# Floors under the planner's due times of the early attention and weight pieces in a fused attention and two-layer feed-forward kernel

## The chip, the cores and the metric

The kernel runs on one core of one Trainium2 chip, in one launch. The time is device microseconds from the first to the last instruction with what lies around them; the figure that counts is the median of several executions.

## The reference

Attention in two directions over `x` (4 batches, 8 heads, 512 positions, 64 wide) and `state` (32 rows), then two feed-forward layers on the 4 x 544 = 2176 tokens of 512 channels. Cut to what matters:

```python
a = softmax(scale * x @ state.T);  xread = a @ state          # per batch and head
a2 = softmax(scale * state @ x.T); sread = a2 @ x
t = concat([xread, sread]) -> (2176, 512)
h = t @ w_in                       # 512 -> 2048
y = (h * tanh(softplus(h))) @ w_out               # 2048 -> 512
yn = y / rms(y) * rms_g
out = (silu(yn @ w_gate) * (yn @ w_val)) @ w_out2 # 512 -> 1536 -> 512
```

## The kernel before

Every product of the two layers is made in float16 pairs: a high part and a low part of each operand, three matmuls for one. The weights come from memory as float32 words in 1 MB halves ("load wi00" is the first half of unit 0 of `w_in`), through two staging buffers in `psm`. Vector and scalar engine turn each into scaled pairs: "hi", "s" (sign, L562), "l" (low words, L567/L569), "join" (L578), "sq" (a sum of squares, L599) for a scale by a tiny ones-matmul ("pow2", L481, six to seven tiny steps on DVE behind it), then "sh" and "sl" (the two halves, L610 by L468/L472 and L612). `w_in` and `w_out` are cut into four units of 512 hidden columns, wi0/wo0 to wi3/wo3. `plain` does one unit.

`attention(b)` makes the two reads of batch b, in two halves of four heads: x comes by eight DMAs of 128 KB (L707), PE transposes the state (L717) and x (L739, into one of four PSUM banks `p`), makes the scores (L752), DVE and ACT make two softmaxes (L761 to L791, the exponentials L768 and L773 on ACT), and PE makes the reads (L799), transposes (L814, L838) and the second product (L825). Batch 2 and 3 are needed late: their reads stand behind most of the first layer.

The first layer is done in groups, g0 to g8 (a batch by some units): `l1` is twelve 512-column matmuls into one bank (L926), followed on ACT by "mish" (L937), then "gh" and "gl" (L941) make the pair for `l2`, six matmuls for each of four column blocks d0 to d3 (L963) of a pair p of hidden blocks. g0 and g1 take unit 0 for batch 0 and 1, g2 and g3 unit 1, g4 and g5 units 2 and 3, g6 to g8 the batches 2, 3 and the state rows (as batch 4, with a scale from "x4"). While g4 and g5 run, `keep` begins to turn the nine units of the second layer's weights into a form that goes back to memory (L1375) through one 2048-word region; the next unit cannot be written into the region before the write out has been read off. The second layer (from about 411 us on) loads these back.

The order is not written by hand. Every step is an `Op` with its engines, cost and buffers; `Plan.order` gives each op a latest time (`chains`), runs a list scheduler by these times (`forward`), takes new latest times from the schedule it got (`backward`), and repeats this up to ten times, keeping the order whose modelled end was earliest. An op's `floor` is a lower bound for its latest time, taken from `P.floor` when the op is made:

```python
    o.floor = None if self.floor is None else self.floor()
    ...
    if o.floor is not None:
        late[o] = max(late[o], o.floor)
```

The second piece stands in `chains` alone; `backward` knows no floors. All engines then run their part of the order strictly in sequence.

Of the kernel before, what the change touches and what calls it, by code (L numbers as in the profile page):

```python
# [36 lines left out]
class Plan:  # L37
# [31 lines left out]
    def op(self, engs, fn, r=(), w=(), tab=None, at=None, reserve=0, lat=0.0, after=(), due=None, name=""):  # L69
        o = Op()  # L70
        o.engs, o.fn, o.tab, o.at, o.due, o.reserve, o.lat, o.name = engs, fn, tab, at, due, reserve, lat, name
        o.floor = None if self.floor is None else self.floor()
        o.succ, o.bufs = [], []
        deps = set(after)
        for n in r:
            if n in self.writer:
                deps.add(self.writer[n])
        for n in w:
            if n in self.writer:
                deps.add(self.writer[n])  # L80
            deps.update(self.readers.get(n, ()))
        for n in r:
            self.readers.setdefault(n, []).append(o)
        for n in w:
            self.writer[n] = o
            self.readers[n] = []
        for n in dict.fromkeys((*r, *w)):
            if n in self.pool_of:
                o.bufs.append(n)
                self.users[n] = self.users.get(n, 0) + 1  # L90
        deps.discard(o)
        o.deps = deps
        self.ops.append(o)
        return o
# [224 lines left out]
def attn_moe_moe_kernel(  # L319
# [23 lines left out]
    P = Plan(nc)  # L343
# [271 lines left out]
    def plain(w, u, m, at, xexp, pool="raw", after=()):  # L615

        def dst(k):
            return m(at + 256 + 512 * k, 512).rearrange("p (a f) -> p a f", a=2)

        def dn(k):  # L620
            return m.names(at + 256 + 512 * k, 512)

        fetch(w, u, dst, dn, pool, after)
        s = norms([(m(at + 256 + 1024 * i, 1024).rearrange("p (a n) -> p a n", a=2), [*dn(2 * i), *dn(2 * i + 1)])
                   for i in range(2)], (w, u), xexp, f"{w}{u}", 2)
        for k in range(4):
            split(m, at, k, s, ((w, u), "s"), f"{w}{u}")
# [322 lines left out]
    def flush():  # L950
        if pending:
            l2(*pending.pop(0))
# [453 lines left out]
    with tc.manual_schedule():  # L1406
        make_identity(nc, ident)
        nc.vector.memset(ones, 1.0)
        nc.vector.memset(rbias, -20.0 * LN2)
        op({"G": 1.6}, lambda e: nc.gpsimd.memset(sb[:, :B // 2], 0.0), w=["state"])  # L1410
        op({"V": 1.6}, lambda e: nc.vector.memset(sb[:, B // 2:], 0.0), w=["state"])
        held = [buf(("held", k), "t") for k in range(6)]
        op({"X": 0.01}, lambda e: None, w=held, name="hold")
        load_state()
        op({"T": 8.0 / 2}, rouse, w=["warm"], name="rouse")
        state_scale()
        attention(0)
        plain("wi", 0, *home["wi", 0], XEXP)
        attention(1)
        plain("wo", 0, *home["wo", 0], XEXP)  # L1420
        for u in range(1, U1):
            plain("wi", u, *home["wi", u], XEXP)
            plain("wo", u, *home["wo", u], XEXP)
        bar = op({"X": 0.01}, lambda e: None, w=["early"], after=list(early_raw), name="early")
        every = list(range(U1))
        group(0, 0, [0], None, 2)
        group(1, 1, [0], None, 3)
        group(2, 0, [1], 2, 2)
        group(3, 1, [1], 3, 3)
        group(4, 0, [2, 3], 2, 0)  # L1430
        flush()
        attention(2, clock[0] + DUE2)
        group(5, 1, [2, 3], 3, 1)
        flush()
        attention(3, clock[0] + DUE3)
        sread_scale(clock[0] + DUE3)
        done = op({"X": 0.01}, lambda e: None, r=held, after=list(att_ops), name="release")
        for w, u, k in (("wg", 0, 0), ("wv", 0, 0), ("wg", 1, 0), ("wv", 1, 1), ("wg", 2, 0), ("wv", 2, 1),
                        ("w2", 0, 1), ("w2", 1, 0), ("w2", 2, 1)):
            keep(w, u, k, [bar, done] if k else [bar])  # L1440
        conv = op({"X": 0.01}, lambda e: None, after=list(early_raw), name="conv")
        opened = []
        load("wg", 1, after=[done, conv])
        load("wv", 1, after=[done, conv])
        for u in range(U2):
            load("w2", u, after=[conv])
        gated_scales()
        group(6, 2, every, None, 2)
        flush()
        rms(0, slots_xe[0], [conv, done])  # L1450
        group(7, B, every, None, B)
        group(8, 3, every, None, 3)
        flush()
        load("wg", 0)
        load("wv", 0)
        opened.append(op({"X": 0.01}, lambda e: None, w=w2m.names(0, 7168), name="open"))
        opened.append(op({"X": 0.01}, lambda e: None, w=psm.names(4608, 1792), after=[conv], name="open"))
        P.floor = lambda: clock[0] - LATER
        gated()
        P.run()  # L1460
# [36 lines left out]
```

## Time and profile before

| | us |
|---|---|
| median of 3 runs (796.73 to 802.6) | 798.7 |
| the profiled execution, its own time | 801.31 |
| its span, first to last instruction | 799.5 |
| PE busy | 772.9 |
| DVE busy | 650.1 |
| ACT busy | 435.8 |
| first `l1` block on PE begins at | 48.02 |

The span is read as PE's time: what PE does not do, and what it does at the lower clock, is what an order can change.

### The profile page before, as it was taken

The page shows a single profiled execution, that of the slowest core. Times are in us where ns is not written, and L with a number is a line of the kernel's source. Part 1 is how long each engine was busy: PE and PEld are TensorE (multiplying, and loading weights), DVE is VectorE, ACT ScalarE, POOL GpSimd, SP SyncE. Part 2 cuts the span into 40 slices and gives each one's busy share as a digit, 9 for nine tenths or more (in the row PEclk, how much of TensorE's full clock was granted, in tenths as well). Part 3 has the DMA queues.
Part 4 walks back from the last instruction along what each step waited for, and adds up shares of the span by engine and source line. Part 5 has one row for each costly group of instructions (what it writes and reads, how often), then busy time and mean ns, then how long its engine had stood idle before and what let it go on. Part 6 is the DMA issues. An engine that isn't in the chain of part 4 may idle for free.

```text
span 799.5 us, 14253 instructions
## 1 busy us (share of the span) xinstructions
PE 772.9 (97%) x5830; PEld 528.0 (66%) x5830; DVE 650.1 (81%) x1332; ACT 435.8 (55%) x802; POOL 1.6 (0%) x7
## 2 busy tenths in 40 slices
PE   7699998999999999999999999999999999999997
PEld 5344454544344444774457588888888889889996
DVE  5989999998978798897689898668975998666671
ACT  6989998854746495776366543315530744122210
POOL 0000000000000000000000000000000000000000
PEclk9689999999999999999999999999999999999999
DMA  8663733202341543605353972368353745275001
GB/s 221 190 182 99 251 97 116 73 2 105 106 155 56 213 157 156 213 15 226 157 198 145 395 275 94 137 233 283 128 217 114 275 158 185 93 294 208 2 1 66
DMA packets 36885, 125.69 MB, mean 157 GB/s; under 512 B 20052, under 2 KB 20052, under 8 KB 30676
## 3 DMA queue, kind: packets, MB, share of 16 engines
q1 hardware_dynamic: 36820, 124.79, 44.0%
q8 instruction: 45, 0.74, 0.4%
q14 instruction: 20, 0.16, 0.1%
HBM read 101.45 MB, written 23.33 MB: 156 GB/s over the span
## 4 chain that ended last, share of the span: by engine, by line
PE 71%; DVE 16%; DMA 6%; ACT 6%; issue 1%; DVEq 0%; ACTq 0%; SPq 0%
PE p L1111 25%; PE a L963 14%; PE p L926 13%; PE a L1195 12%; DMA attm<-kept_wg 3%; PE p L1271 2%; ACT junk L599 1%; DVE g L941 1%; DVE w2m L612 1%; PE a L1309 1%; DVE sxm L562 1%; DVE page L507 1%; PE a L1403 1%; DMA kept_wg<-psm 1%; ACT sxm L567 1%
## 5 line engine op out<-in xcount | busy, mean ns | idle before, releaser
L963 PE MATMUL a<-g,w2m 128*128 128x512 f16 (+1 forms) x960 | 187.1, 349 | 1.1 <-DVE slot L807 0.8
L926 PE MATMUL p<-slot,w 128*128 128x512 f16 (+1 forms) x960 | 186.8, 350 | 0.3 <-ACT tt L937 0.3
L963 PEld LDWEIGHTS <-w2m 128*128 128x128 f16 x960 | 86.0, 99 | 90.9 <-issue 5.6
L926 PEld LDWEIGHTS <-w 128*128 128x128 f16 x960 | 86.3, 99 | 90.3 <-issue 4.1
L1111 PEld LDWEIGHTS <-w 128*128 128x128 f16 x1344 | 131.3, 98 | 17.0 <-issue 0.3
L1123 DVE TENSOR_TENSOR tt<-p,tt 128x512 f32<-128x512 f32 x120 | 82.3, 688 | 31.4 <-PE p L1111 30.4
L1111 PE MATMUL p<-slot,w 128*128 128x256 f16 x768 | 93.3, 273 | 0.0
L468 ACT ACTIVATE w2m<-tt 128x512 f16<-128x512 f32 x45 | 26.9, 623 | 93.0 <-DVE tt L1162 81.1
L1111 PEld LDWEIGHTS <-attm 128*128 128x128 f16 x672 | 65.4, 98 | 10.6 <-DMA attm<-kept_wg 2.2
L1195 PE MATMUL a<-attm,w2m 128*128 128x256 f16 x576 | 66.2, 273 | 0.0
L937 ACT ACTIVATE tt<-p,page 128x512 f32<-128x512 f32 x68 | 45.8, 678 | 32.4 <-PE p L926 32.2
L1195 PEld LDWEIGHTS <-w2m 128*128 128x128 f16 x576 | 56.3, 98 | 6.7 <-issue 0.2
L941 DVE SCALAR_TENSOR_TENSOR g<-tt,page,g 128x512 f16<-128x512 f32 x68 | 50.5, 747 | 2.0 <-ACT g L468 1.3
L1195 PE MATMUL a<-psm,g 128*128 128x256 f16 x432 | 51.9, 273 | 0.0
L1111 PE MATMUL p<-slot,attm 128*128 128x256 f16 x384 | 46.2, 273 | 1.6 <-DMA attm<-kept_wg 1.3
L1195 PEld LDWEIGHTS <-g 128*128 128x128 f16 x432 | 42.2, 98 | 5.6 <-issue 0.6
L1147 ACT ACTIVATE tt<-tt,page 128x512 f32<-128x512 f32 x36 | 25.6, 719 | 35.1 <-DVE tt L1123 35.0
L468 ACT ACTIVATE psm<-psm,page 128x512 f16<-128x512 f32 (+1 forms) x39 | 27.7, 718 | 25.1 <-DVE psm L612 18.0
L1154 DVE TENSOR_TENSOR w2m<-tt,w2m 128x512 f16<-128x512 f32 x48 | 32.2, 686 | 0.9 <-ACT w2m L468 0.6
L1173 DVE TENSOR_TENSOR tt<-tt 128x512 f32<-128x512 f32 x48 | 32.2, 686 | 0.4
L567 ACT ACTIVATE sxm<-psm 128x512 uint16<-128x512 uint16 x41 | 30.9, 776 | 1.1 <-DVE w2m L578 0.6
L612 DVE SCALAR_TENSOR_TENSOR psm<-psm,page 128x512 f16<-128x512 f32 x40 | 29.9, 748 | 1.2 <-ACT psm L468 0.3
(201 smaller groups left out, 1074.2 us busy)
## 6 DMA issues: line engine op xcount, KB each, us to landing
w<-kept_wg SPq DMA_DIRECT2D x8, 1792.0 KB, 7.2
w<-kept_wv SPq DMA_DIRECT2D x8, 1792.0 KB, 7.3
attm<-kept_w SPq DMA_DIRECT2D x12, 1024.0 KB, 7.2
psm<-in_moe_w_out_dram SPq DMA_DIRECT2D x10, 1024.0 KB, 5.0
psm<-in_moe_w_in_dram SPq DMA_DIRECT2D x8, 1024.0 KB, 5.2
attm<-kept_wg SPq DMA_DIRECT2D x4, 1792.0 KB, 8.2
attm<-kept_wv SPq DMA_DIRECT2D x4, 1792.0 KB, 8.7
psm<-in_moe_w_gate_dram SPq DMA_DIRECT2D x6, 1024.0 KB, 5.0
```

What stands on the lines that cost most here:

```text
L468: nc.scalar.activation(o, i, ACTF.Copy, scale=1.0 if scale is None else scale)
L567: nc.scalar.activation(s16[:, :, 0], r16[:, :, 1], ACTF.Copy, scale=2.0 ** -13, bias=2.0 ** -14 - 0.5)
L612: op({"V": v1(512)}, lambda e: nc.vector.scalar_tensor_tensor(lo, f, s, h, ALU.mult, ALU.subtract), r=[*fn_, *hn, sname], w=ln, name=f"sl ...
L926: nc.tensor.matmul(P[ph][:, i * n:(i + 1) * n], part("wi", u, k, a)[:, f * 128:(f + 1) * 128], xh[:, k, b, :], start=m == 0, stop=m == 3 * ...
L937: op({"A": a_ps(512) + 0.09}, lambda e, s=s, ph=ph, ce=ce: nc.scalar.activation(P[s], P[ph], ACTF.Mish, scale=ce), r=[ph, f"ce{c}_{u}"], w ...
L941: op({"V": v1(512) + 0.06}, lambda e, s=s, g=g, u=u: nc.vector.scalar_tensor_tensor(P[g][:, 1, :], P[s], rho[u], P[g][:, 0, :], ALU.mult, ...
L963: nc.tensor.matmul(P[ya[d]][:, :n], part("wo", u, f, a)[:, d * 128:(d + 1) * 128], P[g][:, b, i * n:(i + 1) * n], start=first and m == 0, ...
L1111: nc.tensor.matmul(P[to][:, f * 256:f * 256 + 256], part(w, u, j, a)[:, k * 256 + f * 128:k * 256 + f * 128 + 128], h[:, k, b, :], start=b ...
L1123: op({"V": v1(512) + 0.06}, lambda e: nc.vector.tensor_tensor(P[to], P[bank_], P[a], ALU.add), r=[bank_, a], w=[to], name=f"{w} add")
L1154: op({"V": v1(512)}, lambda e: nc.vector.tensor_tensor(P[g][:, 1, :], P[s], P[g][:, 0, :], ALU.subtract), r=[s], w=[g], name="gl")
L1173: op({"V": v1(512)}, lambda e: nc.vector.tensor_tensor(P[o], P[a], P[b], f), r=[a, b], w=[o], name="gsum")
L1195: nc.tensor.matmul(P[to][:, t * 256:t * 256 + 256], P[g][:, a, o:o + 128], part("w2", u, j, b)[:, f * 256:f * 256 + 256], start=begin and ...
```

## The change

`P.floor` is set while the ops of some early pieces are made. With T0 = 22: attention of batch 0 and the first unit of `w_in` have no floor, batch 1 gets 2, wo0 gets 7, unit 1 gets 22, unit 2 gets 62, unit 3 gets 102, batch 2 gets 102 and batch 3 gets 142 (planner's microseconds). Nothing else is touched; no op is added or taken away, so the two programs differ in the order, in which of two engines takes a piece, and in the activation tables that are loaded in between.

```diff
         attention(0)
         plain("wi", 0, *home["wi", 0], XEXP)
+        P.floor = lambda: T0 + -20
         attention(1)
+        P.floor = lambda: T0 + -15
         plain("wo", 0, *home["wo", 0], XEXP)
+        P.floor = None
         for u in range(1, U1):
+            P.floor = (lambda v: lambda: T0 + v)([0, 40, 80][u - 1])
             plain("wi", u, *home["wi", u], XEXP)
             plain("wo", u, *home["wo", u], XEXP)
+        P.floor = None
...
         flush()
+        P.floor = lambda: T0 + 80
         attention(2, clock[0] + DUE2)
+        P.floor = None
         group(5, 1, [2, 3], 3, 1)
         flush()
+        P.floor = lambda: T0 + 120
         attention(3, clock[0] + DUE3)
+        P.floor = None
```

The queue of SP, which issues all transfers, from its first row on. `attm` and `slot_79` take the x of batch 0 and batch 1, `psm` a half of a weight unit. Before:

```order
L707 DMA attm<-in_x_dram 128x4x64 x5
L671 DMA attm<-in_state_dram 32x8x64 x4
L707 DMA attm<-in_x_dram 128x4x64 x3
L543 DMA psm<-in_moe_w_in_dram 128x2x1024 x2
L707 DMA slot_79<-in_x_dram 128x4x64 x7
```

Now:

```order
L543 DMA psm<-in_moe_w_in_dram 128x2x1024
L707 DMA attm<-in_x_dram 128x4x64
L671 DMA attm<-in_state_dram 32x8x64 x4
L707 DMA attm<-in_x_dram 128x4x64 x7
L543 DMA psm<-in_moe_w_in_dram 128x2x1024
L707 DMA slot_79<-in_x_dram 128x4x64 x8
```

The first half of wi0 has moved ahead of all x and state transfers, the second half stands where it stood.

PE's queue where the x of batch 3 is transposed (L739 x4 into banks p_83 to p_86, after L717 for the state). Before, in g3, with unit 1, the state's transposition one `l1` block earlier:

```order
L926 MATMUL p_86<-slot_77,w_69 128x512
L739 MATMUL p_84<-ident,attm 128x128 x4
L739 MATMUL p_85<-ident,attm 128x128 x4
L739 MATMUL p_83<-ident,attm 128x128 x4
L739 MATMUL p_86<-ident,attm 128x128 x4
L963 LDWEIGHTS w2m
```

Now, behind the first `l1` block of g5 (unit 2, bank p_86) and ahead of the `l2` of g4's last pair, block d1:

```order
L926 MATMUL p_86<-slot_77,w_69 128x512
L717 MATMUL p_83<-ident,attm 128x128 x4
L739 MATMUL p_84<-ident,attm 128x128 x4
L739 MATMUL p_85<-ident,attm 128x128 x4
L739 MATMUL p_86<-ident,attm 128x128 x4
L739 MATMUL p_83<-ident,attm 128x128 x4
L963 LDWEIGHTS w2m
```

The batch's transpositions and all that follows from them have moved from g3 to g5; the third of them takes the bank of the `l1` block just ahead.

ACT's queue at the same g5 block. `psm` is the staging and the region of the units that are kept, L937 is mish. Before, where the mish of that block reads p_85:

```order
L468 ACTIVATE psm<-psm,page_105 128x512
L999 ACTIVATE rms<-slot_76 128x512
L937 ACTIVATE tt<-p_85,page_104 128x512
L468 ACTIVATE psm<-psm 128x2x256 x2
L468 ACTIVATE psm<-psm,page_68 128x2x256 x2
```

Now, where it reads p_86:

```order
L937 ACTIVATE tt<-p_85,page_103 128x512
L468 ACTIVATE psm<-psm 128x2x256
L999 ACTIVATE rms<-slot_76 128x512
L468 ACTIVATE psm<-psm,page_68 128x2x256
L937 ACTIVATE tt<-p_86,page_104 128x512
L468 ACTIVATE attm<-p_83 128x512
L468 ACTIVATE tt<-p_84 128x512
```

The hi step of wv0 (psm<-psm) and the gain step behind it (psm<-psm,page_68) stood behind that mish and now stand ahead of it. The whole ACT queue holds 26 table loads now, 24 before.

## Rows read from the trace of the kernel before

**Rows 1.** The page: PE's busy time, and the granted clock in 40 slices (tenths).

```profile
PE 772.9 (97%) x5830; PEld 528.0 (66%) x5830; DVE 650.1 (81%) x1332; ACT 435.8 (55%) x802; POOL 1.6 (0%) x7
...
PEclk9689999999999999999999999999999999999999
```

**Rows 2.** Busy time by stage: stretch, length, each engine's busy us (instructions), clock, DMA share, GB/s.

```profile
8.60:46.90 38.30, 26.68 (x154) 13.60 (x153) 36.36 (x88) 36.19 (x76) 0.00 (x0) 0.70 0.82 226
46.90:176.10 129.20, 123.77 (x773) 60.82 (x772) 123.13 (x329) 113.96 (x199) 0.00 (x0) 0.98 0.35 115
176.10:191.90 15.80, 15.80 (x75) 7.16 (x74) 15.37 (x59) 8.11 (x12) 0.00 (x0) 1.00 0.00 0
```

**Rows 3.** Who PE waited for after 55 us: total, times, longest.

```profile
PE p L739 <- ACT tt L937: 2.6, 2, 1.5
PE p L481 <- ACT junk L599: 1.9, 1, 1.9
```

**Rows 4.** Timeline of PE around its two longest waits: start, us, instruction, [idle before].

```profile
127.64 2.42 PE L963 MATMUL a<-g,w2m 128*128 128x512 f16 x6
...
206.56 5.34 PE L963 MATMUL a<-g,w2m 128*128 128x512 f16 x24
213.76 0.39 PE L481 MATMUL p<-page,ones 128*128 128x8 f32 x2 [1.86 <-ACT junk L599]
214.01 7.03 PE L926 MATMUL p<-slot,w 128*128 128x512 f16 x24
```

**Rows 5.** Timeline of SP's queue: the first weight loads and the first kept unit.

```profile
8.21 1.13 SPq L543 DMA_DIRECT2D psm<-in_moe_w_in_dram  x2
...
191.92 0.35 SPq L1375 DMA_DIRECT2D kept_wg<-psm  x1
```

**Rows 6.** Timeline of DVE: its first work, wi0's last split, the first kept unit's scale.

```profile
8.59 0.69 DVE L470 COPY tt<-p 128x512 f32<-128x512 f32 x1 [6.51 <-PE p L739]
...
46.16 0.74 DVE L612 SCALAR_TENSOR_TENSOR w<-w,page 128x512 f16<-128x512 f32 x1
...
176.09 0.10 DVE L489 TENSOR_REDUCE page<-p 128x1 f32<-128x8 f32 x1
```

**Rows 7.** Timeline of ACT: its first work, a table load, the hi step of wv0.

```profile
9.02 0.60 ACT L468 ACTIVATE tt<-p 128x512 f32<-128x512 f32 x1 [7.01 <-PE p L739]
...
97.98 1.28 ACT L286 ACT_TABLE_LOAD   x1
99.27 0.69 ACT L768 ACTIVATE attm<-p,page 128x512 f32<-128x512 f32 x1
...
198.29 1.23 ACT L468 ACTIVATE psm<-psm 128x512 f32<-128x512 f32 x2 [2.50 <-DMA kept_wg<-psm]
```

**Rows 8.** Timeline of PE: first `l1`, batch 3's pieces, g4's last pair, g6's first block.

```profile
48.02 2.75 PE L926 MATMUL p<-slot,w 128*128 128x512 f16 x12
...
130.21 1.94 PE L752 MATMUL p<-tt,attm 128*64 128x512 f32 x8
...
145.31 1.04 PE L814 MATMUL p<-ident,attm 128*128 128x128 f32 x8
...
150.28 1.10 PE L825 MATMUL p<-attm 128*32 128x64 f32 x64
...
172.75 0.28 PE L481 MATMUL p<-page,ones 128*128 128x8 f32 x2
...
194.91 2.75 PE L963 MATMUL a<-g,w2m 128*128 128x512 f16 x12
...
239.73 2.75 PE L926 MATMUL p<-slot,w 128*128 128x512 f16 x12
```

**Rows 9.** DMA issues by line: count, KB each, median us from issue to landing.

```profile
psm<-in_moe_w_in_dram SPq DMA_DIRECT2D x8, 1024.0 KB, 5.2
```

**Rows 10.** Groups of DVE from 176 to 192 us: count, busy us, mean ns.

```profile
L612 DVE SCALAR_TENSOR_TENSOR psm<-psm,page 128x512 f16<-128x512 f32 x8 | 6.0, 745 | 0.0
...
L472 DVE TENSOR_SCALAR psm<-psm,page 128x512 f16<-128x512 f32 x1 | 0.5, 477 | 0.0
```

## The prediction, made before the change was run

> **What bounds the kernel now.** I read the page's busy line first. PE is busy 772.9 of 799.5 us [rows 1], so an order can only win what PE idles, 26.6 us, and what it does at the lower of its two clock levels. The digits of the granted clock say where that is: below full in the first slices, hardly anywhere after [rows 1]. Then the table by stage. From 8.6 to 46.9 us DVE is busy 36.4 of 38.3 us and ACT 36.2, while PE has 26.7 us of work, at a mean clock of 0.70 [rows 2]: here the two elementwise engines set the pace. From 46.9 to 176.1 PE is busy 123.8 of 129.2 and DVE 123.1 [rows 2]; both are full, and PE's 5.4 us of waits are the places where DVE or ACT came late. The list of waits names the largest: 2.6 us in two waits for a bank that a mish (L937) had yet to free, and 1.9 us for the squares of wv0 (L599) [rows 3]. The timeline adds what they cost after their end. Six matmuls behind the first took 2.42 us, where 24 take 5.34, so six 1.3: 1.1 us lost. The 24 behind the second took 7.03 instead of 5.34: 1.7 us lost, at the lower clock [rows 4]. The two places cost 3.7 and 3.6 us. After 240 us PE has next to no wait, and from the second batch of the second layer on PE's order is unchanged. So the case is decided ahead of g6, whose first block starts at 239.73 [rows 8], and I add up what moves that start.
>
> **Part one, the head.** wi0's first half was issued at 8.21 behind all of batch 0 [rows 5]. Now it is first; with 5.2 us to landing [rows 9] it is there at about 6. DVE did nothing before 8.59 and ACT nothing before 9.02 [rows 6, 7], waiting for PE's first transpositions, so two signs, a low, two joins on DVE (2.5 us) and three steps on ACT fit into the idle stretch. Against it: the state's squares now stand behind these on ACT, and PE and DVE wait for the scale made of them (pow2 x), about 0.5 us. The DVE work ahead of wi0's last split is the same (40.2 us now, 39.9 before, the order's steps at the trace's durations). The split started at 46.16 and the first `l1` at 48.02 [rows 6, 8]. I take a lead of 2.0 us. Bounds: 2.5, the whole of what fits; and 3 the other way, if the x transfers behind the megabyte leave DVE idle for half of its 5.2 us.
>
> **Part two, batch 3 leaves g3.** Its four transpositions with two bank waits are gone from there: 3.7 us of PE. DVE has 14 full-size steps of batch 3, their short ones and x4's scale less ahead of the first kept unit (12.5 us), and 8.0 us of conversions and small products that used to come later: 4.5 us less, which at 123.1 busy of 129.2 [rows 2] and with the overlap of neighbours is 4.2 us. PE had 7.5 us less. So PE cannot keep all of what it gains: DVE now is the later of the two, and I follow DVE. It read the scale of wg0 at 176.09 [rows 6]; with the 2.0 of the head and these 4.2 it reads it at 169.9.
>
> **Part three, batch 3 arrives in g5.** This is the place I weigh most. The third transposition there needs the bank of the `l1` block just ahead, so it waits for that block's mish, and that mish stands on ACT behind wv0's hi and gain steps. Hi overwrites the region that wg0 is written out from, so it waits for that transfer. Nothing of this chain hung on PE before: the hi step waited 2.50 us [rows 7], and the mish had gone ahead. The chain, link by link: DVE has a scale, eight splits at 0.745, four halves at 0.477 [rows 10], three gl steps of the split's form and a product to do before wg0 is complete, 11.2 us summed, 10.0 with the overlap of neighbours (before, 59 instructions and 15.8 us stood there [rows 2, 10]). The write out took from 191.92 to the start of hi at 198.29, 6.4 us [rows 5, 7]. Then hi on DVE for the other slice, an evacuation, a join, ACT's gain and mish: 3.4. Together 19.8, and the third transposition starts at 189.7. Two transpositions at 0.5 (the L814 row has two such in 1.04 [rows 8]) follow, and the second quarter of g4's last `l2` pair starts at 190.7. Before, it started at 194.91 [rows 8]: 4.2 us ahead there. From it to g6 PE has what it had, plus batch 3's scores, transpositions and second products, 1.94 + 1.04 + 1.10 = 4.1 us [rows 8], minus the wait for wv0's squares with its clock, 3.6. That wait goes because wg0 leaves the region some ten microseconds of PE's order sooner relative to the same pow2. A new wait of 2 to 5 us costs the clock again as the old one did: 1.7 [rows 4]. So 4.2 - 4.1 + 3.6 - 1.7 = 2.0 us ahead at g6.
>
> Bounds of the new wait: nothing, if DVE is as close to PE as before, when it read wg0's scale 3.3 us behind PE (172.75 against 176.09 [rows 6, 8]); and, from the other side, as long as the same stretch took before, 191.92 - 176.09 = 15.8 instead of 10.0. I take 10.0, since the tiny products and the softmax steps that filled the difference stand elsewhere now.
>
> **Part four, the tables.** Two more loads of an activation table on ACT. A load is 1.28 us, and the next exponential starts 0.01 after its end [rows 7]; 2.6 us on an engine that is busy 55% [rows 1], and they lie behind the mish that PE waits for: nothing. If the cover is gone they cost their 2.6. The Trainium skill, ScalarE: Activation LUTs, section What ACT_TABLE_LOAD costs, says that a drain of about 1.4 us comes with each switch, 2.66 us together; by that the two would be 5.3 us (an estimate from the page), still behind the same cover. The trace shows no such drain: load and exponential touch.
>
> **After g6** the orders differ by the places of five scales and one rms matmul, with the same blocks around them. Two scales (of w2's units 0 and 2) stand 4 and 5 us earlier on PE; I take nothing, with up to 2 us for each as a bound.
>
> **The sum.** The profiled execution took 801.31 us with a span of 799.5; 2.0 less is 799.3. It lay 2.6 above the median of the runs, 798.7. Against that median the forecast is 796.7 us.
>
> **Rivals.** First, DVE is not the later one, and the bank in g5 is free in time. For it: ACT was busy only 8.1 of 15.8 us there [rows 2], so a mish that may start is done within a microsecond. Against it: both engines were full up to there. Then all three gains stay, 2.0 + 3.7 + 3.6 = 9.3: 789.4 us. Second, the other side: the chain through the region is slower than the 10.0 I give it. If wg0 takes DVE the 15.8 us of before, and the head gives nothing, the third transposition starts 7.8 us later than forecast, PE waits 10 us where it waited for nothing, and the sum is 5.8 behind: 804.5. If the x transfers also hold the head up by 3 us, it is 807.5. The point from which it decides is a chain more than 2.0 us longer than mine. Third, the change does not do what it says: floors act in the first of up to ten rounds only, later rounds know nothing of them. The order bears this out in part: batch 2's transpositions still stand ahead of the first `l1`, though batch 2 has a floor of 102. Then it is another order of the same planner, with waits of the same size at other places: 798.7, within 3.
>
> **How the numbers follow.** I give the forecast 0.45, the first rival 0.2, the second 0.2, the third 0.15. A difference of 1%, 8 us, is about what a measurement of this kernel tells from none; the old runs alone spread over 6. Of the first rival nearly all lies past 1% faster, and a little of the forecast's tail; of the second, its worse half lies past 1% slower. That makes 0.2 faster, 0.65 same, 0.15 slower. The range reaches down to 788, past the first rival, and up to 806, past the second's first price; what is left out is the case in which head and chain both go wrong, and a gain beyond the listed waits.
>
> **What would show it.** Part one is right if DVE's first step of wi0 starts near 6 us and the first `l1` by 46.5; wrong if that starts at 48 or later. Part two, if there is no bank wait of PE in g3 and g2's and g3's blocks run without a gap. Part three, if the third of the four L739 blocks in g5 waits 2 to 6 us for a mish on L937, ACT's hi step ahead of it waits for the transfer of wg0, and the lower clock shows behind it; wrong if the transpositions run on. The pow2 of wv0 should wait for nothing. The forecast as a whole fails if PE's waits between 50 and 240 us sum to over 12 us, or if a wait of several us turns up after 240, where I expect none.

## The result, and the profile after

The changed kernel took 805.71 us in the median of 10 runs (803.17 to 806.78), the kernel before, run between them, 798.42 (796.73 to 802.6). The ratio is 1.008, with a 95% interval from 1.0064 to 1.0095. It became 0.8% slower, clear of the interval, where I had forecast 2 us faster. The profiled execution took 804.91 us, with a span of 803.1.

The page after, its busy line and the granted clock, against [rows 1]:

```profile
PE 774.1 (96%) x5830; PEld 526.7 (66%) x5830; DVE 656.1 (82%) x1344; ACT 429.9 (54%) x792; POOL 1.6 (0%) x7
...
PEclk9689999999999999999999999999999999999999
```

PE's busy time rose by 1.2 us and its idle time from 26.6 to 29.0. The table by stage (as in [rows 2]: stretch, length, busy us of PE, its weight loads, DVE, ACT and POOL with instructions, granted clock, DMA share, GB/s) says where. After:

```profile
8.60:46.90 38.30, 27.62 (x160) 14.59 (x160) 33.41 (x77) 34.46 (x73) 0.00 (x0) 0.72 0.78 204
46.90:176.10 129.20, 123.82 (x698) 57.58 (x695) 124.54 (x352) 108.60 (x186) 0.00 (x0) 0.99 0.36 115
176.10:191.90 15.80, 15.22 (x81) 7.96 (x79) 10.14 (x18) 5.84 (x10) 0.00 (x0) 1.00 0.51 198
240.00:410.00 170.00, 168.69 (x1068) 88.22 (x1067) 143.12 (x286) 105.62 (x227) 0.00 (x0) 1.00 0.42 157
410.00:420.00 10.00, 7.70 (x46) 4.82 (x45) 9.51 (x25) 5.88 (x17) 0.00 (x0) 0.83 0.30 126
```

The last two stretches of the kernel before, which the prediction had not looked at:

```profile
240.00:410.00 170.00, 170.00 (x1077) 89.21 (x1076) 141.98 (x284) 107.05 (x225) 0.00 (x0) 1.00 0.40 150
410.00:420.00 10.00, 10.00 (x77) 7.32 (x76) 9.53 (x24) 8.09 (x23) 0.00 (x0) 1.00 0.55 225
```

Up to 240 us nothing speaks for a loss. From 240 to 410 PE stands for 1.3 us where it never stood, and in the ten microseconds behind 410 for 2.3, with a granted clock of 0.83 in place of 1.00, so a part of them at the lower of the two levels, 1.2 GHz. The list of waits after 55 us names the same thing, against [rows 3]:

```profile
PE p L481 <- ACT junk L599: 3.5, 2, 2.3
PE p L814 <- DVE attm L472: 2.0, 1, 2.0
PE p L926 <- ACT tt L937: 1.2, 1, 1.2
...
PE p L838 <- ACT attm L468: 1.0, 1, 1.0
```

PE's timeline at these places and at those of [rows 4, 8]. The first row stands ahead of the first `l1`, those at 140 to 156 us are in g4, that at 189.81 is the third transposition in g5, the last four are the scales of w2's units 0 and 2 and the two blocks behind the latter:

```profile
41.91 0.63 PE L739 MATMUL p<-ident,attm 128*128 128x128 f32 x4 [1.77 <-DMA attm<-in_x_dram]
...
49.17 1.19 PE L926 MATMUL p<-slot,w 128*128 128x512 f16 x4
...
140.28 2.75 PE L926 MATMUL p<-slot,w 128*128 128x512 f16 x12 [1.23 <-ACT tt L937]
149.32 0.66 PE L814 MATMUL p<-ident,attm 128*128 128x128 f32 x4 [1.97 <-DVE attm L472]
156.38 0.33 PE L838 MATMUL p<-ident,attm 128*128 128x128 f32 x1 [0.98 <-ACT attm L468]
...
189.81 1.15 PE L739 MATMUL p<-ident,attm 128*128 128x128 f32 x8 [0.58 <-ACT tt L937]
190.80 1.46 PE L963 MATMUL a<-g,w2m 128*128 128x512 f16 x6
...
237.44 2.75 PE L926 MATMUL p<-slot,w 128*128 128x512 f16 x12
...
376.77 0.39 PE L481 MATMUL p<-page,ones 128*128 128x8 f32 x2 [1.16 <-ACT junk L599]
...
413.15 0.39 PE L481 MATMUL p<-page,ones 128*128 128x8 f32 x2 [2.31 <-ACT junk L599]
...
414.70 2.74 PE L963 MATMUL a<-g,w2m 128*128 128x512 f16 x6
417.24 1.91 PE L1111 MATMUL p<-slot,w 128*128 128x256 f16 x12
```

At g6's first block the changed kernel is 2.3 us ahead of the trace before (237.44 against 239.73 [rows 8]); at its end it is 3.6 behind. The 5.9 us between are two waits of 1.2 and 2.3 us, and 1.7 at the lower clock behind the second: six matmuls in 2.74 us where six take 1.46, twelve in 1.91 where twelve take 1.47 (the granted clock from 414.7 to 419.0 us was 0.60 in the mean). That is 5.2; the rest lies in small pieces that I did not follow.

The same two scales in the kernel before, on PE, and the last squares that each of them waits for, on ACT:

```profile
381.20 0.29 PE L481 MATMUL p<-page,ones 128*128 128x8 f32 x2
...
416.35 0.29 PE L481 MATMUL p<-page,ones 128*128 128x8 f32 x2
```

```profile
379.81 0.19 ACT L599 ACTIVATION_READ_ACCUMULATOR junk<-attm 128x1 f32 x1
...
414.23 0.19 ACT L599 ACTIVATION_READ_ACCUMULATOR junk<-attm 128x1 f32 x1
```

They were there to be read: the squares ended 1.2 and 1.9 us ahead of the scales (379.81 + 0.19 against 381.20, 414.23 + 0.19 against 416.35), and the change puts the scales 3.9 and 5.2 us of PE's work earlier (the blocks that stood between 377.32 and 381.20, and between 411.12 and 416.35, now stand behind them).

### The profile page after: what moved, and what is told of

Read it like the earlier page. It is cut to its first block, busy times and chain, and to the rows that moved or that the text cites. A ratio compares the mean times of both kernels' runs of the same rounds, so it can differ in the third digit from the quotient of the medians.

```text
span 803.1 us, 14259 instructions
## 1 busy us (share of the span) xinstructions
PE 774.1 (96%) x5830; PEld 526.7 (66%) x5830; DVE 656.1 (82%) x1344; ACT 429.9 (54%) x792; POOL 1.6 (0%) x7
## 4 chain that ended last, share of the span: by engine, by line
PE 50%; DVE 28%; ACT 11%; DMA 9%; issue 2%; DVEq 0%; ACTq 0%; SPq 0%
PE p L1111 23%; PE a L1195 12%; PE a L963 6%; PE p L926 4%; ACT junk L599 2%; DMA attm<-kept_wg 2%; DVE attm L612 2%; DVE g L941 2%; PE p L1271 2%; ACT sxm L567 1%; DVE psm L612 1%; DVE sxm L562 1%; DVE attm L472 1%; DVE tt L1123 1%; DVE w L612 1%
## 5 line engine op out<-in xcount | busy, mean ns | idle before, releaser
L926 PE MATMUL p<-slot,w 128*128 128x512 f16 (+1 forms) x960 | 184.9, 347 | 1.2 <-ACT tt L937 1.2
L1123 DVE TENSOR_TENSOR tt<-p,tt 128x512 f32<-128x512 f32 x120 | 82.2, 686 | 33.8 <-PE p L1111 32.9
L1111 PEld LDWEIGHTS <-attm 128*128 128x128 f16 x672 | 65.4, 98 | 10.6 <-DMA attm<-kept_wg 1.7
L937 ACT ACTIVATE tt<-p,page 128x512 f32<-128x512 f32 x68 | 45.6, 674 | 27.1 <-PE p L926 27.0
L612 DVE SCALAR_TENSOR_TENSOR psm<-psm,page 128x512 f16<-128x512 f32 x40 | 29.9, 747 | 1.5 <-ACT psm L468 0.2
```

The source lines that it names most:

```text
L612: op({"V": v1(512)}, lambda e: nc.vector.scalar_tensor_tensor(lo, f, s, h, ALU.mult, ALU.subtract), r=[*fn_, *hn, sname], w=ln, name=f"sl ...
L926: nc.tensor.matmul(P[ph][:, i * n:(i + 1) * n], part("wi", u, k, a)[:, f * 128:(f + 1) * 128], xh[:, k, b, :], start=m == 0, stop=m == 3 * ...
L937: op({"A": a_ps(512) + 0.09}, lambda e, s=s, ph=ph, ce=ce: nc.scalar.activation(P[s], P[ph], ACTF.Mish, scale=ce), r=[ph, f"ce{c}_{u}"], w ...
L1111: nc.tensor.matmul(P[to][:, f * 256:f * 256 + 256], part(w, u, j, a)[:, k * 256 + f * 128:k * 256 + f * 128 + 128], h[:, k, b, :], start=b ...
L1123: op({"V": v1(512) + 0.06}, lambda e: nc.vector.tensor_tensor(P[to], P[bank_], P[a], ALU.add), r=[bank_, a], w=[to], name=f"{w} add")
```

## The experiments

All kernels have the new floors in a field of their own, so that the planner can be run with them and without them, and an order can be put together from two: up to a named PE block from one, the rest from the other.

```diff
+    def both(self, head, tail, cut):
+        first, rest = self.planned(head), self.planned(tail)   # True: with the new floors
+        k = next(i for i, (o, e) in enumerate(first) if o.name == cut and e == "T")
+        made = {o for o, e in first[:k]}
+        return first[:k] + [(o, e) for o, e in rest if o not in made]
...
-        for _, o, e in self.order():
+        for o, e in self.both(True, False, "l1 g6 u0 [0]"):
```

Ratios are to the kernel before, run in the same job, with 95% intervals. "T" is PE in these lines, and `scales_later` moves a scale matmul, with what hangs on it where that would come too soon, behind the n-th PE step after it. Line numbers of the experiments are shifted against the tables above; what a line does is said where it matters.

| kernel | order | median us | ratio |
|---|---|---|---|
| head_new | new to g6, then old | 799.22 | 1.0009 [0.9995, 1.0024] |
| head_old | old to g6, then new | 803.95 | 1.0070 [1.0051, 1.0089] |
| w20_alone | new to g8's last `l1`, then old | 800.43 | 1.0020 [1.0002, 1.0037] |
| w22_alone | old to g8's last `l1`, then new | 804.49 | 1.0064 [1.0040, 1.0088] |
| scales_later | new, w2's scales 2 and 4 PE steps later | 808.96 | 1.0130 [1.0112, 1.0149] |
| second_later | new, batch 2's transpositions later | 808.72 | 1.0125 [1.0103, 1.0148] |
| w20_later | new, w2 unit 0's scale 2 steps later | 804.12 | 1.0063 [1.0039, 1.0088] |
| w22_two | new, w2 unit 2's scale 2 steps later | 804.41 | 1.0084 [1.0070, 1.0098] |
| both_two | new, both 2 steps later | 803.67 | 1.0076 [1.0063, 1.0090] |
| seam_two | w22_two, and ACT's emptying earlier | 805.04 | 1.0080 [1.0059, 1.0102] |
| seam_three | both_two, and ACT's emptying earlier | 804.65 | 1.0072 [1.0053, 1.0091] |
| seam_add | seam_three, and DVE's add earlier | 807.19 | 1.0122 [1.0098, 1.0145] |
| wv0_later | old, wv0's scale 2 steps later | 803.53 | 1.0054 [1.0035, 1.0073] |
| wv0_one | old, wv0's scale 1 step later | 797.06 | 0.9990 [0.9978, 1.0003] |
| wv0_wg1_one | old, wv0's and wg1's 1 step later | 798.60 | 1.0009 [0.9997, 1.0021] |
| nudged | floors of the units 2 us later | 801.05 | 1.0031 [1.0017, 1.0046] |
| batches_only | floors of batches 2 and 3 alone | 809.25 | 1.0135 [1.0115, 1.0156] |
| nudged_g7 | nudged to g7, then old | 794.58 | 0.9954 [0.9936, 0.9971] |

**Where the loss lies.** Theory A: behind g6, at w2's scales. Theory B: in the head, where PE waits for the x of batch 2. Four kernels: the order cut at g6 in both ways, the scales alone put back, and batch 2's transpositions moved behind the first `l1`.

```diff
+        for o, e in self.both(True, False, "l1 g6 u0 [0]"):    # head_new
+        for o, e in self.both(False, True, "l1 g6 u0 [0]"):    # head_old
+        for o, e in self.scales_later(self.planned(True), [("pow2 ('w2', 0)", 2), ("pow2 ('w2', 2)", 4)]):
+        for o, e in self.second_later(self.planned(True)):
```

> The changed order up to the first block of g6, and from there the steps that are left in the order of before. Theory A (the loss lies behind g6, where two scales of the w2 units stand earlier on PE): the changed trace is 2.2 us ahead of before at the first block of g6 and 3.6 behind at the end, so this kernel keeps the 2.2: about 796 us against 798.4 before, PE waits on L481 after 300 us under 1 us. Theory B (the loss lies in the changed head and in batch 2 and 3 among g4 and g5, and the profiled execution of before was a late one): about 803 to 806, as the changed kernel.

> The order of before up to the first block of g6, and from there the steps that are left in the changed order. Theory A: it loses what the changed kernel loses behind g6 and has nothing of its lead, 5.8 us by the two traces, so 804 to 806; PE waits on L481 for squares near 377 and 411 us, over 3 us together. Theory B: as before, 798 to 800.

> The changed order with the scale of w2's unit 0 put two PE steps later and that of unit 2 four PE steps later, nothing else. Theory A: the two waits of 1.2 and 2.3 us go, and with them the low clock behind the second (1.7 us): 5.2 us less than the changed kernel's 805.7, about 800.5. Theory B: within 1 us of 805.7.

> The changed order with batch 2's transpositions, which stand ahead of the first l1 on PE and wait there for their x, put behind the first l1. Theory A: the first l1 begins about 3 us earlier, near 46, but DVE sets the pace to g5, so 0 to 2 us of it are left at g6 and at the end: 804 to 805.7. Theory B: the head's loss of 1.2 us against before turns into a gain that lasts: 802 to 803.

The tail alone costs a ratio of 1.0070, the head alone nothing that can be measured: the place that A named is shown, and B falls. A's 796 for head_new was missed all the same, since there was no lead to keep. The traces say the same without the head: from g6's first block to the end pass 559.8 us in the kernel before and in head_new, and 565.7 and 566.2 in the changed kernel and in head_old. But with the scales put back the kernel was slower still, which neither theory had expected. In scales_later PE no longer waited for squares and stood at the first quads of the second layer instead, for banks that ACT (L503, a step that empties a bank) and DVE (L1158, an add) freed late. Four steps were also too many for DVE, which stood 2.55 us for unit 2's scale:

```profile
415.56 1.47 PE L1146 MATMUL p<-slot,w 128*128 128x256 f16 x12 [3.13 <-ACT tt L503]
...
424.23 2.54 PE L1146 MATMUL p<-sxm,w 128*128 128x256 f16 x12 [3.15 <-DVE tt L1158]
```

In second_later the first `l1` started at 48.3 us, no earlier than in the kernel before, and the kernel fell 8 us behind before's trace by its end, against what both theories said. PE no longer stood for the x of batch 2 there; it stood for squares that ACT makes:

```profile
44.67 0.59 PE L516 MATMUL p<-page,ones 128*128 128x2 f32 x2 [5.07 <-ACT junk L634]
```

**Which of the two scales.** Theory A, each scale carries its own wait; theory C, the steps behind the scales fit only as a whole.

```diff
+        for o, e in self.both(True, False, "l1 g8 u3 [3]"):    # w20_alone
+        for o, e in self.both(False, True, "l1 g8 u3 [3]"):    # w22_alone
+        for o, e in self.scales_later(self.planned(True), [("pow2 ('w2', 0)", 2)]):
```

> The changed order up to the last l1 block of g8, from there the order of before: of the two scales that stand earlier behind g6, only that of w2's unit 0 is in it. Theory A, each early scale costs what PE waits there and the clock behind it: unit 0's wait was 1.2 us with no fall of the clock in the changed kernel, the head gave nothing measurable, so 1 to 1.5 us over the order that is new only up to g6: 800 to 800.7. Theory C, the loss is not in the two scales but at the seam into the second layer, whose two sides only fit where both come from the same order: then this cut is as bad as the other one, 803 or more.

> The order of before up to the last l1 block of g8, from there the changed order: only the scale of w2's unit 2 stands early. Theory A: the wait of 2.3 us, the clock behind it (1.7), together 3.5 to 4 over before: 802 to 803. Theory C: 800 or less here if unit 0 is what does it, and 805 or more if a seam alone costs.

> The changed order with the scale of w2's unit 0 two PE steps later, where it stood before, and unit 2's left early. Theory A: the 1.2 us of unit 0's wait come back: 804 to 805. Theory C: as slow as with both moved (808 to 809), since then any step of the planned order that is moved without the rest blocks DVE or ACT.

Unit 0's place costs little: 800.43 with it, as A said, and 804.12 when it alone is put back. That is in A's range too, but not clear of the change (1.0063 against 1.0080, with intervals that overlap), and the wait at unit 2 grew from 2.31 to 2.76 us. Unit 2's end of the order holds the rest, more than A gave it: in w22_alone PE stood ready 2.3 us sooner than in the changed kernel (408.5 against 410.8) and waited 3.6 us, not 2.3, with 1.7 lost at the lower clock behind. The squares ended only 1.1 sooner: they do not follow PE.

**What stands behind unit 2's scale.** I took the limits away one after another. First the scale alone, two PE steps later with every other queue untouched; then also ACT's step that empties the bank of the second layer's first quads, ahead of the rms steps (theory E); then also the first add of the second layer, ahead of unit 2's steps on DVE (theory H).

```diff
+        for o, e in self.scales_later(self.planned(True), [("pow2 ('w2', 2)", 2)]):    # w22_two
+        for o, e in self.scales_later(self.planned(True), [("pow2 ('w2', 0)", 2), ("pow2 ('w2', 2)", 2)]):
...
+    def seam(self, made):        # wg c0 u0 A11 and its emptying go behind "l2 g8 p3 d1"
+        first = next(o for o, e in made if o.name == "wg c0 u0 A11" and e == "T")
+        empty = next(o for o, e in made if o.name == "wg a1" and first in o.deps)
...
+    def add_first(self, made):   # the add of wg c0 u0 S2 goes ahead of DVE's pow2 ('w2', 2)
```

> The changed order with one PE instruction pair moved: the scale matmul of w2's unit 2 stands two PE steps (2.6 us) later; every other queue is word for word the same. In the changed kernel PE waited 2.3 us for its squares and lost 1.3 to 1.7 at the lower clock behind, and DVE read the scale only 2 us after it was made. Theory A, that wait is PE's own loss and the cover of 2 us behind it is real: 3.5 to 4 back, 801.7 to 802.3. Theory C, what stands behind the scale has no slack, as when it stood four steps later: PE waits for a bank in the next quads instead, 805 or more.

> The same for both scales of w2, units 0 and 2, each two PE steps later. Theory A: unit 0's 1.4 comes back as well, and PE reaches unit 2's scale that much sooner with its squares where they were, so 0.2 to 0.4 of wait is left: 800.2 to 801, no more than 2 above the kernel before. Theory C: 804 or more.

> The changed order with two instructions moved: the scale matmul of w2's unit 2 two PE steps later, as before, and on ACT the step that empties the bank of the second layer's first quads one to three places earlier, ahead of the rms steps, where the kernel before had it ahead of the last square. Theory E, the loss at the seam is ACT's queue, squares first and the emptying last, so that PE waits for the one or for the other: now it waits for neither, 3.6 to 4 come back, 801.7 to 802.3. Theory C, the whole run of steps behind the scale is too tight, whatever is moved: 804 or more, with a wait of 2 us or more in the next quads.

> The same, and the scale of w2's unit 0 two PE steps later. Theory E: unit 0's 1.4 as well, 800.2 to 801, as near to the kernel before as the order whose tail is all from before (800.4). Theory C: 803 or more.

> The changed order with four things where the kernel before had them: the scales of w2's units 0 and 2 two PE steps later, ACT's emptying of the first bank ahead of the rms steps, and now the first add of the second layer on DVE ahead of the small steps for unit 2's scale, in place of behind five of its halves. With the first three moved, PE waited 2.7 us for that add. Theory H, three limits stand right behind one another at the seam (squares, emptying, add), and what is won is the least of them: with all three out of the way 3.5 to 4 come back, 800.5 to 801.5. Theory C, DVE is full from 407 to 428 us and has to be waited for wherever its steps stand: 804 or more, with the wait in the quads behind.

None of the five won anything back that can be measured: their ratios run from 1.0072 to 1.0122, the change had 1.0080. Theories A, E and H fall. C named the waits rightly, though two times came out a little under its bounds (804.41 for 805, 803.67 for 804). PE's wait for unit 2's squares was gone or small (0.56 us at most), but another wait came up in its place. w22_two waited 2.58 us for the emptying, seam_two 2.68 for the add, seam_add 4.88 for the next add. PE's timelines of these three, one after another:

```profile
414.41 0.28 PE L516 MATMUL p<-page,ones 128*128 128x8 f32 x2
417.27 2.49 PE L1146 MATMUL p<-slot,w 128*128 128x256 f16 x12 [2.58 <-ACT tt L503]
```

```profile
420.95 1.47 PE L1155 MATMUL p<-sxm,w 128*128 128x256 f16 x12 [2.68 <-DVE tt L1167]
```

```profile
423.82 4.31 PE L1166 MATMUL p<-slot,w 128*128 128x256 f16 x24 [4.88 <-DVE tt L1178]
```

What they have in common is DVE. From 407 to 428 us, before and then after (the columns of [rows 2]):

```profile
407.00:428.00 21.00, 21.00 (x152) 14.58 (x151) 20.25 (x50) 16.97 (x35) 0.00 (x0) 1.00 0.45 156
```

```profile
407.00:428.00 21.00, 18.70 (x122) 12.24 (x121) 20.24 (x49) 14.31 (x33) 0.00 (x0) 0.92 0.24 88
```

DVE is full in both, 20.25 and 20.24 of 21 us. What it does differs: the adds (L1123) that free PE's banks, before and then after, up to 425 us:

```profile
416.38 0.68 DVE L1123 TENSOR_TENSOR tt<-p,tt 128x512 f32<-128x512 f32 x1
419.83 0.69 DVE L1123 TENSOR_TENSOR tt<-p,tt 128x512 f32<-128x512 f32 x1
421.75 1.29 DVE L1123 TENSOR_TENSOR tt<-p,tt 128x512 f32<-128x512 f32 x2
```

```profile
420.95 0.68 DVE L1123 TENSOR_TENSOR tt<-p,tt 128x512 f32<-128x512 f32 x1
424.60 0.68 DVE L1123 TENSOR_TENSOR tt<-p,tt 128x512 f32<-128x512 f32 x1
```

Four adds against two, the first 4.6 us later. Why it is later can be read from where DVE starts: at the sign step (L562) of the half of w2's unit 2 that was loaded last, before and then after:

```profile
406.98 0.80 DVE L562 TENSOR_SCALAR sxm<-attm 128x512 uint16<-128x512 uint16 x2 [1.50 <-DMA attm<-in_moe_w_out_dram]
```

```profile
404.95 0.80 DVE L562 TENSOR_SCALAR sxm<-attm 128x512 uint16<-128x512 uint16 x2 [3.33 <-DMA attm<-in_moe_w_out_dram]
```

From there to the first add DVE works without a wait, 9.4 us in the old queue and 16.0 in the new one, where two gl steps, unit 2's scale and five of its halves stand ahead of the add. The 16.0 (to 16.1) are the same in ten traces, whatever was moved on PE or ACT: the changed kernel, head_old, w20_later, w22_two, both_two, seam_two, seam_three, second_later, nudged and batches_only. The 9.4 are the same in before, head_new, wv0_one, wv0_wg1_one and nudged_g7. And the end comes 381.6 to 383.3 us behind that add in 18 of the 20 traces; the two others are scales_later, 383.7, and seam_add, which moved the add itself.

The halves of w2's staged unit that L612 makes on DVE go the other way, from 414 to 428 us, before and then after (operation, count, ns, first and last start):

```profile
L612 DVE SCALAR_TENSOR_TENSOR attm<-attm,page x4: 740/744/752, 420.4 to 427.5; 128x512 f16<-128x512 f32 x4
```

```profile
L612 DVE SCALAR_TENSOR_TENSOR attm<-attm,page x6: 741/742/751, 417.7 to 427.9; 128x512 f16<-128x512 f32 x6
```

The changed tail has DVE split w2's unit 2 early, in a stretch where DVE has no time to give, ahead of the adds that PE needs. As long as the first add stands 16.0 us behind the load, PE cannot go on sooner: waits of 2.6 to 4.9 us came up, and at which semaphore was a matter of which step was moved. This is read from the traces; a kernel with DVE's queue alone put back was not made, and seam_add, which moved one add, brought PE's wait to the next.

**Do the units keep their own pace?** Theory D: the second layer's units pass through their staging one by one, so PE that comes sooner only waits at the next scale. Tried on the kernel before, whose one large wait behind 55 us is wv0's [rows 3].

```diff
+        for o, e in self.scales_later(self.planned(False), [("pow2 ('wv', 0)", 2)]):    # wv0_later
+        for o, e in self.scales_later(self.planned(False), [("pow2 ('wv', 0)", 1)]):    # wv0_one
+        for o, e in self.scales_later(self.planned(False), [("pow2 ('wv', 0)", 1), ("pow2 ('wg', 1)", 1)]):
```

> The order of before with the scale of wv0 two PE steps later, so that PE does not wait for its squares (1.9 us, 1.7 of clock behind it) in the first layer. Theory A, such a wait is PE's own loss: 2 to 3.5 less than before, 795 to 796.5. Theory C: what stands behind the scale on DVE and ACT, the halves of wv0 and the steps that free PE's banks, comes later by the same two steps and PE waits for those: the same as before or slower, 798.5 to 803.

> The order of before, the scale matmul of wv0 one PE step (2.6 us) later, nothing else moved on any queue. It removes a wait of 1.9 us and the 1.7 of clock behind it. Theory A, PE's own loss: 3.5 back, 795. Theory D, the kept units run on a clock of their own, from region to write out to next load, and PE that comes sooner waits at the next of them: wg1's squares ended 1.4 ahead of PE in the kernel before, so of 3.5 gained 2.1 is waited out there and 1.7 lost at the lower clock behind it: 798 to 799, no change.

> The order of before, the scale matmuls of wv0 and of wg1 each one PE step later. Theory D: now the wait at wg1 has its 2.6 us of cover as well, the 3.5 us hold past g6, and the time is 794.5 to 796, below both kernels, unless the next kept unit takes it. Theory A says the same number, but for the kernel with wv0 alone too; if that one shows no change and this one 3 less, D is shown.

PE at the next scale that waits, in wv0_later, wv0_one and wv0_wg1_one:

```profile
252.98 0.60 PE L516 MATMUL p<-page,ones 128*128 128x8 f32 x2 [4.38 <-ACT junk L634]
```

```profile
247.89 0.39 PE L516 MATMUL p<-page,ones 128*128 128x8 f32 x2 [0.99 <-ACT junk L634]
```

```profile
337.24 0.39 PE L516 MATMUL p<-page,ones 128*128 128x8 f32 x2 [1.31 <-ACT junk L634]
```

Two steps later is too late, and slower than C's upper bound of 803 as well: wv0 leaves the region later (its write is issued at 230.26 us, 227.01 before), wg1 is loaded later (239.33, 235.76 before), and PE stands 4.4 us at wg1's scale. One step later is free, but a part of what it wins is waited out at wg1; with wg1's scale moved too the next wait comes at wv2's. Neither is faster by more than its interval. So D's mechanism is shown, a wait that comes up again at the next scale, but its 3 us for the last kernel are not.

**Is it the floors, or any other order?** Theory F: floors give the planner another start, and where it ends is accident. Theory G: such floors bring the early scales with them.

```diff
-            P.extra = (lambda v: lambda: T0 + v)([0, 40, 80][u - 1])
+            P.extra = (lambda v: lambda: T0 + v)([2, 42, 82][u - 1])    # nudged
...
-        P.extra = lambda: T0 + -20
-        P.extra = lambda: T0 + -15
-            P.extra = (lambda v: lambda: T0 + v)([0, 40, 80][u - 1])
+        # batches_only: nothing in place of these three
```

> The change with the floors of units 1 to 3 at 24, 64 and 104 instead of 22, 62 and 102, nothing else. Theory F, the floors set only where the planner's rounds start from, and which late scale is tight falls out by accident: the order differs in hundreds of places from the changed one, and the time lies anywhere from 797 to 806, with waits at other places than at w2's units 0 and 2. Theory G, floors of this kind lead to a packed seam as such: 804 to 807 with the same two waits.

> The floors of batch 2 and batch 3 alone; none for the first unit, batch 1 and the units. Theory F: another order again, 797 to 806, with the waits at w2 present or not by accident. Theory G, what pushes the weights of the second layer early is batch 3 moved behind them: the two waits at w2 are here as well, 803 to 806, though the head is that of before.

Both theories hold a part. The time goes from 801 to 809 with 2 us on three floors, or half of the floors left away: the spread of F, past its upper end and past G's in one case, below G's lower end in the other. But in both, as in the changed kernel, PE waits at both of w2's scales, as G said. nudged is the clearest: at g6 it is 10.6 us ahead of before's trace, at its end 2.3. Of the 8.3 that it gave back, 3.9 went at unit 0's scale:

```profile
370.71 0.39 PE L495 MATMUL p<-page,ones 128*128 128x8 f32 x2 [1.98 <-ACT junk L613]
370.96 2.29 PE L977 MATMUL a<-g,w2m 128*128 128x512 f16 x6
373.04 3.65 PE L940 MATMUL p<-slot,w 128*128 128x512 f16 x12
```

**A version that beats both.** nudged's head with the tail of the kernel before.

```diff
+        for o, e in self.both(True, False, "l1 g7 u0 [0, 1, 2, 3]"):    # floors of nudged
```

> The order that the floors at 24, 64 and 104 give, up to the first block of g7, and the order of before from there. That head was 8.8 us ahead of before's trace at g7 and gave 6.4 of it back at w2's scales. Theory D, from wg1's scale to w2's last needed squares the units take 161 to 164 us in every order, and only an order whose scales stand as late as before's has the room: PE comes to unit 2's scale when its squares end, 407.6, and 7 to 8.8 hold to the end: 794 to 796.5, below both kernels. Theory C: the seam fits its own head only, and the lead is waited out there as well: 798 to 801.

It took 794.58 us, a ratio of 0.9954 [0.9936, 0.9971], inside the range that D gave. PE at wg1's scale and at that of w2's unit 2:

```profile
245.52 0.39 PE L495 MATMUL p<-page,ones 128*128 128x8 f32 x2 [1.05 <-ACT junk L613]
...
409.26 0.29 PE L495 MATMUL p<-page,ones 128*128 128x8 f32 x2
```

Its lead over before's trace was 7.1 us at g8 and 8.0 at the end. Read with the other traces this sizes the tail. From wg1's scale to the last square of w2's unit 2 pass 163.0 us in the kernel before (251.38 to 414.42), 161.4 in the changed one (251.69 to 413.1), 161.7 here. PE's own work between the two scales is 165.0 us in the old tail (251.38 to 416.35, no wait), but 157.7 in the changed one (from 251.69 until PE stood ready at 410.84, less 1.4 lost at unit 0). Room of 2 us became a lack of 3.7, and that is what was lost: 1.4 at unit 0 and 2.3 at unit 2.

## Why the prediction was wrong, point by point

**The step that failed** is "After g6": the scales of w2's units 0 and 2 "stand 4 and 5 us earlier on PE; I take nothing, with up to 2 us for each as a bound". They took 5.2 us with the clock, more than the 4 of both bounds together, and head_old shows the tail alone to be worth the whole loss. Two things were left out. The squares of each scale end 1.2 and 1.9 us ahead of it in the trace before, so 3.9 and 5.2 us of advance had to give waits of about 2.7 and 3.3 by that trace (1.2 and 2.3 came), and [rows 4] had a price of the clock behind a wait of that kind. And I compared PE's order only. The same move put DVE's halves ahead of its adds, in a stretch where DVE is full, and the first add came 16.0 us behind the last load of w2's unit 2 in place of 9.4; that is why moving the scales alone back won nothing. The fail condition that I had set, a wait of several us after 240, was right, but the sum had no term for it. That 805.7 us still lies inside the range, whose upper end of 806 was set by the second rival, is luck.

**Part one** failed too: no lead in the head. DVE's first step of wi0 came at 6.23 us, as forecast, but the first `l1` began at 49.17, past the 48 that I had set as wrong. One trace decides little here: in ten executions of the changed head it began between 47.45 and 50.61 us, 48.7 in the mean, and in six of the old head between 47.40 and 49.18, 48.4 in the mean. PE stood for the x of batch 2, whose transpositions are ahead in its queue (1.77 us at 41.91), but second_later shows that this is not what holds the block: without it PE stood 5.07 us for squares on ACT. What makes these late I did not follow.

**Part two** had its direction right and its size too small: there was no wait in g3, and DVE read wg0's scale at 167.99 us where 169.9 was forecast, 8.1 earlier than before. As the head gave none of these, what left the stretch ahead of it was worth about twice the 4.2 that I took.

**Part three** had its amount right by luck and its cause wrong. DVE reads the scale, and SP issues the write of wg0:

```profile
167.99 0.17 DVE L489 TENSOR_REDUCE page<-p 128x1 f32<-128x8 f32 x1
```

```profile
180.44 0.36 SPq L1375 DMA_DIRECT2D kept_wg<-psm  x1
```

The chain from there took 12.5 us to the write, not 10.0, then 6.4 to hi on ACT (186.82), as forecast, and 3.0 to the third transposition: 21.8 in place of 19.8, from a start that was 1.9 earlier. The third transposition began at 189.81 (forecast 189.7) and the `l2` block behind it at 190.80 (190.7), but PE waited 0.58 us there, not 2 to 6. PE came late because it had stood 4.2 us in g4, at and around batch 2's pieces (the rows at 140 to 156 us), which I had not costed. The lower clock that I had put behind a wait here did not show either: six matmuls took 1.46 us. The wait for wv0's squares went, as forecast.

**The sum at g6** read 2.3 us ahead (2.0 forecast), and most of that was not the change. wv0's wait was there in two other executions of the old head, but without the fall of the clock behind it, and they began g6 2.4 and 2.8 us ahead of the trace before. Ten executions of the changed head are 2.9 ahead in the mean. That leaves 0.1 to 0.5 us for it against those two, 1.1 against the mean of all three, and head_new measures none. So 3.6 for wv0's place was a term mis-sized: the wait of 1.7 to 1.9 in all three traces, the 1.7 of clock in one. I had noted that the profiled execution lay 2.6 us above its median and did not ask where.

**Part four** holds as far as the trace goes: a load of 1.28 us at 196.38 stands between an ACT step that ends at 196.36 and an exponential at 197.68, without a gap, as in [rows 7]. What the two added loads cost by themselves no run shows.

**The rivals.** The second named the right side and nearly the right time, 804.5, but not how it came about. The chain through the region was indeed 2.0 us longer than mine, the point from which this rival was to decide, but it started 1.9 earlier, PE waited 0.58 us for it in place of 10, and the kernel was ahead at g6. The third, another order of the same planner, is what nudged and batches_only bear out, but its price of "798.7, within 3" was too narrow: the orders tried lie from 801 to 809.

What stays open: why the head gains nothing from its earlier start, and whether a tail with the scales early is worth having if DVE's queue there is written anew. Both would need more than single steps moved.

## What to carry to other kernels

Where an instruction is moved earlier, read when its producer ended in the trace before: what is left of the advance after that gap is a wait, to be costed even if the blocks around it look the same. Compare the queues of every full engine at the place, not only of the one that sets the time; where taking one wait away brings out another just behind it, look for the engine that is busy throughout. And with a planner, cut its orders at a block and join them: nudged's head was worth having only with the old tail.

## What the runs showed of the hardware that I had not expected

The lower clock behind a wait of PE does not follow from the wait's length alone. Behind 1.86 us the next 24 matmuls took 7.03 us in the kernel before [rows 4], at a mean granted clock of 0.76 from 214 to 221 us. Behind 1.76 us at the same scale in w22_alone 15 took 3.40, at a granted clock of 1.00:

```profile
212.66 0.39 PE L495 MATMUL p<-page,ones 128*128 128x8 f32 x2 [1.76 <-ACT junk L613]
212.90 3.40 PE L940 MATMUL p<-slot,w 128*128 128x512 f16 x15
```

Behind 2.58 us w22_two ran its next two blocks of twelve in 2.49 and 2.16 us (granted clock 0.59 from 417.3 to 421.5), while behind 2.68 and 3.13 us seam_two and scales_later ran theirs in 1.47 (1.00). No run here separates what else decides.
